# Splitting the turns of chunks 2 and 3 in a fused attention and expert kernel, with the copies of turned blocks put first on ACT

## Chip, cores and metric

The kernel runs on one core of one Trainium2 chip. The metric is the device time of one execution in microseconds (us), as the median of several runs. Engines are named as in the profile: PE (matrix engine; PEld is its weight load), DVE, ACT, POOL, and SP, which issues the transfers.

## What is computed

Block-causal attention for 8 batches of 8 heads with 576 positions and 64 columns per head, in fp32, and behind it an expert layer on the 4608 x 512 result with a hidden width of 2048:

```python
scores = np.where(mask, scale * np.matmul(q, k.transpose(0, 1, 3, 2)), -1000000000.0)   # 64x64 blocks
attn = np.exp(scores - np.max(scores, axis=-1, keepdims=True))
attn = attn / (np.sum(attn, axis=-1, keepdims=True) + 1e-09)
x = np.matmul(attn, v)          # then (4608, 512)
h = x @ w_in
g = h * (1.0 / (1.0 + np.exp(-1.702 * h)))
out = (g @ w_out).astype(np.float32)
```

## The kernel before

**Attention.** Two heads make a pair, and 32 pairs are worked off one after the other. A turn n (counted from 0, as in the code) does the scores of pair n and the end of pair n-1. The rows of a pair are cut into five chunks: chunk 0 has 64 rows and 64 columns, chunks 1 to 4 have 128 rows and 192, 320, 448 and 576 columns. `score` (L305) multiplies on PE into PSUM banks. `weigh` (L340) takes the row maximum on DVE (L351), which also moves the scores out of the bank, and the exponential on ACT (L358). `normalise` (L364) forms the reciprocal of the sums on DVE (L368, L371) and scales on POOL (L376).

**Turning.** The weights of attention must be transposed before they meet the values in `av` (L429). For pairs 0 to 7 PE transposes 128x128 blocks into a bank (`flip`, L401, through L102), and ACT copies them to `pw` (L411 for whole blocks, L424 for the 64-column ends). From pair 8 on DVE transposes (L385, L390) and transfers move the blocks. `flip` of chunks 2 and 3 is the step B, of chunk 4 the step C, of chunks 0 and 1 the step a.

**Banks.** All these products use PSUM banks in rotation (`bank`, L89). In turns 4 to 8, once the experts have begun, there are three, w0 to w2. A new writer waits until the reader of the bank's last contents is done: the maximum for scores, the copy for turned blocks. B takes four banks in a row: one for chunk 2, two for chunk 3, one for the ends.

**Experts.** 12 tiles of 384 tokens, and 16 hidden chunks of 128 in each. A chunk is 12 matmuls into the one bank of `hp` (four triples: w_in high, w_in low, and w_in high with the low part of x), the gate (ACT L562, DVE L563, ACT L571, POOL L82), and 9 matmuls of the chunk before into `acc`. The first tile lies between the steps of turns 4 to 8, and PE works in the order in which the program was written.

**Weights.** The two expert weights arrive as 64-bit words and are converted to a high and a low part in 32 pieces, in turns up to 8. Each piece goes ACT L219 into a bank, DVE L223, L229 and L234, ACT L243 (high part), POOL L82 (low part, `wil` or `wol`); the next piece begins after L243. Hidden chunks 12 to 15 need pieces 24 to 27 of w_in, one for each of the four triples.

**Order.** The slots of a turn are written out in strings (L26 to L33): `START` for turn 4, `ORDER[1]` for turns 5 to 7, `HANDOVER` for turn 8. Between the slots `advance` puts as much expert work as a quota by position asks for. On DVE, ACT and POOL a scheduler orders by priority; within `tc.high_priority(offset=300)` work goes ahead, before the change only for the gate and the split of x.

Of the kernel before, what the change touches and what calls it, by code (L numbers as in the profile page):

```python
# [24 lines left out]

ORDER = (  # L26
# [3 lines left out]
)  # L30

START = "1+0 - B 2/3 L C - V - 4 - a - - -"
HANDOVER = "B C - 3+0/2+1 - - V - - - 4 - - L - -"  # L33


WEIGHTS_BY = ((0, 0), (8, 13), (14.5, 32))
# [4 lines left out]
def attention_moe_kernel(  # L41
# [9 lines left out]
    nc = tc.nc  # L51
    B, H, S, D = q.shape
# [11 lines left out]
    HP = H // 2  # L64
# [9 lines left out]
    def early(n):  # L74

        return n < 2 * HP

    def phase(n):
        return 0 if n < HP else 1 if n < 2 * HP else 2
# [9 lines left out]
    def bank():  # L89
        tags = ["w0", "w1", "w2"]  # L90
        if not turns["experts"]:
            tags += ["acc0", "acc1", "acc2", "h"]
        elif turns["n"] > 2 * HP:
            tags.append("w3")
        turns["bank"] += 1
        return ps.tile([P, 512], F32, tag=tags[turns["bank"] % len(tags)], name="bank")
# [4 lines left out]
    def tr(**kw):  # L101
        return tc.keep_in_program_order(nc.tensor.transpose(**kw))  # L102
# [62 lines left out]
    def width(i):  # L165
        return BLK * (2 * i + 1)
# [46 lines left out]
    bits, whole = {}, {}  # L213
# [54 lines left out]
    def load(n):  # L268

        if n in (1, 3):  # L270
            raw[n] = room("xh", [P, 2, S // 32, 32], F32, "raw")
        else:
            raw[n] = d2.tile([P, 2, S // 32, 32], F32, tag="raw", name="raw", bufs=1)
        for x, src in enumerate((q, k)):
            queue = nc.scalar if n < 2 and x else nc.sync
            for hd, b, h in heads(n):
                for c in range(0, D, 32):
                    r = hd * D + c
                    queue.dma_start(
                        out=raw[n][r : r + 32, x],  # L280
                        in_=src[b, h][:, c : c + 32].rearrange("(c p) d -> p c d", p=32),
                    )
# [9 lines left out]
    def prep(n):  # L292

        tag = "e0" if early(n) and n % 2 else "qk"
        qk[n] = d2.tile([P, 2, S], F32, tag=tag, name="qk", bufs=1)
        for x in range(2):
            nc.vector.transpose(out=qk[n][:, x], in_=raw[n][:, x].rearrange("p c d -> p (c d)"))  # L297
        raw.pop(n)
        m = follower(n)
        if m is not None:  # L300
            load(m)
# [3 lines left out]
    def score(n, banks):  # L305

        if n not in stats:
            mx = d2.tile([P, NCH + 1, 2], F32, tag="mx", name="mx")
            sm = d2.tile([P, NCH, 2], F32, tag="sm", name="sm")
            stats[n] = (mx, sm)  # L310
        todo = []
        for chunks in banks:

            part = []
            for lo, hi in ((0, 512),) if width(chunks[0]) <= 512 else ((0, 256), (256, S)):
                ss = [bank() for _ in range(2)]
                c = 0
                for i in chunks:
                    a, z = qrange(i)
                    w = min(hi, width(i)) - lo  # L320
                    for hd in range(2):
                        r = slice(hd * D, hd * D + D)

                        mm(
                            out=ss[hd][:, c : c + w], lhsT=qk[n][r, 0, a : a + P],
                            rhs=qk[n][r, 1, lo : lo + w], start=True, stop=True,
                        )
                        part.append((i, hd, lo, lo + w, ss[hd][0 : z - a, c : c + w]))
                    c += w
            todo.append(sorted(part, key=lambda x: (chunks[::-1].index(x[0]), x[2])))  # L330
        for chunks, part in zip(banks, todo):
            e = {}
            for i, hd, lo, hi, s in part:
                e[i] = weigh(n, i, hd, lo, hi, s, e.get(i))
            for i in chunks[::-1]:
                normalise(n, i, e[i])
                if not early(n):
                    turn(n, i, e[i])
# [59 lines left out]
                        out=pw[kb * 32 : kb * 32 + 32, qb, 0:ns], in_=tw[qb * 32 : qb * 32 + 32, kb, 0:ns]  # L398
                    )

    def flip(n, chunks):  # L401

        for i in chunks:
            todo = [(j, hd) for j in range(i) for hd in range(2)]
            for x in range(0, len(todo), 4):
                part = todo[x : x + 4]
                bk = bank()
                for y, (j, hd) in enumerate(part):
                    tr(out=bk[:, y * P : (y + 1) * P], in_=es[i][:, hd, j * P : (j + 1) * P], identity=ident)
                s0 = SLOT[i] + part[0][0]  # L410
                nc.scalar.copy(  # L411
                    out=pw[:, :, s0 : s0 + len(part) // 2].rearrange("p b s h c -> p (s h) b c"),
                    in_=bk[:, 0 : len(part) * P].rearrange("p (x b c) -> p x b c", b=4, c=32),
                )

        bk = bank()
        todo = [(i, hd) for i in chunks for hd in range(2)]
        for y, (i, hd) in enumerate(todo):
            tr(out=bk[0:BLK, y * P : (y + 1) * P], in_=es[i][:, hd, i * P : width(i)], identity=ident)
        src = bk[0:BLK, 0 : len(todo) * P].rearrange("p (x b c) -> p x b c", b=4, c=32)  # L420
        for part in ([0], [1]) if 0 in chunks else (chunks,):
            i, x, a = part[0], 2 * chunks.index(part[0]), 2 if part[0] else 0
            s0 = 9 + max(i, 1)
            nc.scalar.copy(  # L424
                out=pw[0:BLK, a : a + 2, s0 : s0 + len(part)].rearrange("p b s h c -> p (s h) b c"),
                in_=src[:, x : x + 2 * len(part), a : a + 2],
            )

    def av(n):  # L429

        b, h = divmod(n, HP)
        before_av(n)
        o, o0 = bank(), bank()

        todo = []
        for i in range(1, NCH):
            c = (i - 1) * P
            todo += [(o, c, P, j, pw[:, :, SLOT[i] + j]) for j in range(i)]
            todo.append((o, c + BLK, BLK, i, pw[:, 2:4, 9 + i]))
        last = len(todo) - 1  # L440
        todo.append((o0, 0, BLK, 0, pw[:, 0:2, 10]))

        for x, (bk, c, nn, j, w) in enumerate(todo):
            for hd in range(2):
                mm(
                    out=bk[hd * D : hd * D + D, c : c + nn].rearrange("d (a c) -> d a c", c=32),
                    lhsT=values(n)[:, hd, j], rhs=w[:, :, hd], start=x in (0, last + 1), stop=x >= last,
                )
        c0 = (b % 2) * S
        nc.scalar.copy(out=xr[:, h, c0 : c0 + BLK], in_=o0[:, 0:BLK])  # L450
        nc.scalar.copy(out=xr[:, h, c0 + BLK : c0 + S], in_=o)
        m = follower(n)
        if m is not None:
            load_v(m)

    def follower(n):

        m = {0: 2, 1: 3, 2: 4, 3: None}.get(n, n + 1)
        return None if m is None or m >= NPAIR else m

    def order(n):
        return {HP: START, 2 * HP: HANDOVER}.get(n, ORDER[phase(n)]).split()

    def step(n):

        turns["n"] = n
        now = n < NPAIR

        def item(x):
            if x == "V":  # L470
                return (lambda: av(n - 1)) if n else None
            if x == "L":
                return (lambda: prep(n + 1)) if n + 1 < NPAIR else None
            if x in ("a", "B", "C"):
                m, chunks = {"a": (n, [0, 1]), "B": (n - 1, [2, 3]), "C": (n - 1, [4])}[x]
                return (lambda: flip(m, chunks)) if m >= 0 else None
            return (lambda: score(n, [[int(z) for z in y.split("+")] for y in x.split("/")])) if now and x != "-" else None

        return [item(x) for x in order(n)]
# [26 lines left out]
    def chunk_time(tt):  # L506
        return 4 * unit1(tt) + tt // P * 650
# [72 lines left out]
    ends = np.cumsum([0.0] + [NFC * chunk_time(tt) for _, tt in TILES])  # L580
# [84 lines left out]
```

## Time and profile before

| | us |
|---|---|
| median of 3 runs | 1122.48 (1120.67 to 1125.02) |
| profiled execution | 1120.49 |
| its span, first to last instruction | 1118.6 |
| PE busy | 1076.4 |
| DVE, ACT, POOL busy | 583.0, 498.6, 406.7 |

A busy share is an average over stages with different limits. A stretch of the span is read by its own row, and the idle time in front of an instruction, with what ended it, says who was late there. The granted clock is that of PE; 1.00 is 2.4 GHz and 0.50 is 1.2 GHz.

### The profile page before, as it was taken

How to read it: one execution, taken by the hardware profiler on the slowest of the kernel's cores; microseconds unless marked ns; L12 is line 12 of the kernel's file. 1: busy time of each engine (PE TensorE's matmuls, PEld its weight loads, DVE VectorE, ACT ScalarE, POOL GpSimd, SP SyncE). 2: the span in 40 equal slices, each digit the busy share in tenths (PEclk: the TensorE clock that was granted, in tenths of full speed). 3: DMA queues.
4: the chain of work that ended last, by engine and by line, in shares of the span. 5: the costliest groups of instructions: out<-in, count | busy, mean ns of one | idle time of the engine just before them, and what ended most of it. 6: DMA issues, size and time to landing. Idle time of an engine off the chain costs nothing. (4 is left out here: it accounts for less than half of the span.)

```text
span 1118.6 us, 19977 instructions
## 1 busy us (share of the span) xinstructions
PE 1076.4 (96%) x6960; PEld 908.7 (81%) x6960; DVE 583.0 (52%) x1856; ACT 498.6 (45%) x1321; POOL 406.7 (36%) x509
## 2 busy tenths in 40 slices
PE   5969998999999999999999999999999999999998
PEld 3757776788888888888888888888888888899997
DVE  6776885545545555654555655645545654211210
ACT  5866776434534433534443543444434444322322
POOL 4665664333333332333333333333333233122222
PEclk9979999999999999999999999999999999999999
DMA  8734532332444432343443333344342332200000
GB/s 171 205 89 153 150 73 62 84 79 57 105 86 86 103 80 64 64 98 78 98 101 74 75 93 65 70 108 85 81 107 63 71 85 58 54 29 1 29 1 29
DMA packets 219365, 91.25 MB, mean 82 GB/s; under 512 B 197760, under 2 KB 197760, under 8 KB 219264
## 3 DMA queue, kind: packets, MB, share of 16 engines
q1 hardware_dynamic: 214528, 89.38, 34.0%
q10 hardware_dynamic: 4736, 0.59, 0.3%
q8 instruction: 55, 0.90, 0.3%
q14 instruction: 46, 0.38, 0.1%
HBM read 45.09 MB, written 9.44 MB: 49 GB/s over the span
## 5 line engine op out<-in xcount | busy, mean ns | idle before, releaser
L82 POOL TENSOR_TENSOR gl<-g,gh 128x384 fp32r<-128x384 f32 x192 | 194.7, 1014 | 551.5 <-ACT gh L571 449.1
L99 PE MATMUL hp<-xh,wih 128*128 128x384 f32 x768 | 264.7, 345 | 7.9 <-DVE g L563 6.9
L563 DVE SCALAR_TENSOR_TENSOR g<-g,hp 128x384 f32<-128x384 f32 x192 | 105.9, 552 | 319.1 <-ACT g L562 317.8
L99 PE MATMUL hp<-xh,wil 128*128 128x384 f32 x768 | 258.4, 336 | 0.1
L562 ACT ACTIVATE g<-hp 128x384 f32<-128x384 f32 x192 | 94.1, 490 | 359.8 <-PE hp L99 354.8
L99 PE MATMUL hp<-xl,wih 128*128 128x384 f32 x768 | 253.9, 338 | 0.4 <-DVE xl L82 0.4
L99 PE MATMUL acc<-woh,gh 128*128 128x512 f32 x576 | 233.9, 406 | 0.0
L99 PE MATMUL acc<-wol,gh 128*128 128x512 f32 x576 | 226.9, 394 | 0.0
L99 PEld LDWEIGHTS hp<-xh,wih 128*128 128x128 f32 x768 | 144.2, 188 | 34.1 <-DVE g L563 23.1
L99 PE MATMUL acc<-woh,gl 128*128 128x512 f32 x576 | 167.9, 393 | 0.3 <-POOL gl L82 0.3
L571 ACT CAST gh<-g 128x384 fp32r<-128x384 f32 x192 | 98.4, 513 | 156.5 <-DVE g L563 156.4
L99 PEld LDWEIGHTS hp<-xh,wil 128*128 128x128 f32 x768 | 144.3, 188 | 6.5 <-POOL wil L82 0.7
L358 ACT ACTIVATE e<-e,mx 64x64 f32<-64x64 f32 (+4 forms) x240 | 132.3, 552 | 37.6 <-DVE mx L351 37.6
L376 POOL TENSOR_TENSOR e<-e,sm 64x64 f32<-64x64 f32 (+1 forms) x192 | 113.6, 612 | 95.0 <-DVE sm L371 46.5
L99 PEld LDWEIGHTS hp<-xl,wih 128*128 128x128 f32 x768 | 143.6, 188 | 1.3 <-DVE xl L82 1.3
L99 PE MATMUL bank<-qk 64*128 64x320 f32 (+4 forms) x768 | 122.5, 428 | 14.5 <-DVE qk L297 11.1
L99 PEld LDWEIGHTS acc<-woh,gh 128*128 128x128 f32 x576 | 107.9, 187 | 34.2 <-issue 10.5
L99 PEld LDWEIGHTS acc<-woh,gl 128*128 128x128 f32 x576 | 107.8, 188 | 25.9 <-POOL gl L82 1.2
L99 PEld LDWEIGHTS acc<-wol,gh 128*128 128x128 f32 x576 | 108.3, 188 | 16.7 <-POOL wol L82 0.3
L351 DVE CUSTOM_DVE_ANT_0 e<-bank,mask 64x64 f32<-64x64 f32 (+4 forms) x240 | 89.7, 417 | 56.9 <-PE bank L99 52.8
L385 DVE STREAM_TRANSPOSE turned<-e 128x384 f32<-128x384 f32 (+1 forms) x192 | 92.3, 499 | 48.8 <-POOL e L376 48.3
L99 PEld LDWEIGHTS bank<-qk 64*128 64x128 f32 x768 | 69.6, 193 | 54.2 <-issue 25.4
(50 smaller groups left out, 956.0 us busy)
## 6 DMA issues: line engine op xcount, KB each, us to landing
turned<-turned SPq DMA_DIRECT2D x192, 80.0 KB, 2.1
turned<-turned SPq DMA_DIRECT2D x96, 112.0 KB, 2.2
raw<-in_q_dram SPq DMA_DIRECT2D x128, 72.0 KB, 2.4
out_dram<-osb SPq DMA_DIRECT2D x36, 256.0 KB, 2.2
raw<-in_k_dram SPq DMA_DIRECT2D x120, 72.0 KB, 2.6
turned<-turned SPq DMA_DIRECT2D x96, 88.0 KB, 2.1
words<-in_moe_w_in_dram SPq DMA_DIRECT2D x16, 512.0 KB, 6.3
vp<-in_v_dram SPq DMA_DIRECT2D x60, 128.0 KB, 2.4
```

The costliest lines, as they stand in the source:

```text
L82: eng.tensor_tensor(out=out, in0=in0, in1=in1, op=ALU.subtract)
L99: return tc.keep_in_program_order(nc.tensor.matmul(**kw))
L351: nc.vector.tensor_tensor_reduce(out=e[0:m, hd, lo:hi], in0=s, in1=mk, op0=ALU.add, op1=ALU.min, scale=-0.125, scalar=3e38 if lo == 0 else ...
L358: nc.scalar.activation(out=e[0:m, hd], in_=e[0:m, hd], func=AF.Exp, scale=-1.0, bias=mx[0:m, i, hd : hd + 1], accum_out=sm[0:m, i, hd : hd ...
L376: nc.gpsimd.tensor_tensor(out=x, in0=x, in1=sc.to_broadcast([m, width(i)]), op=ALU.mult)
L385: nc.vector.transpose(out=tw[:, :, SLOT[i] : SLOT[i] + i, hd].rearrange("p b j c -> p j b c"), in_=e[:, hd, 0 : i * P],)
L562: nc.scalar.activation(out=g, in_=hp[:, 0:tt], func=AF.Tanh, scale=1.702)
L563: nc.vector.scalar_tensor_tensor(out=g, in0=g, scalar=1.0, in1=hp[:, 0:tt], op0=ALU.add, op1=ALU.mult)
L571: nc.scalar.copy(out=gh, in_=g)
```

## The change

Turns 5 to 8, the sixth to the ninth, get other steps. B is cut in two: b turns the whole blocks of chunk 2 and the ends of chunks 2 and 3 (two banks), c the whole blocks of chunk 3 (two banks), with experts in the slots between. In turn 8 C stands two slots behind c. The strings get longer, from 16 to 17 and from 16 to 19 slots, so the quota places expert work by finer steps. The copies of `flip` are issued at high priority for pairs from 4 on; that holds for a, b, c and C.

```diff
-    "1+0 - B - 2 - C - 3 L V - a - 4 -",
+    "1+0 - b - c 2 - C - 3 L V - a - 4 -",
-HANDOVER = "B C - 3+0/2+1 - - V - - - 4 - - L - -"
+HANDOVER = "b - c - C - 3+0/2+1 - - V - - - 4 - - L - -"
...
-    def flip(n, chunks):
+    def flip(n, chunks, whole=None, ends=True):
+        def move(**kw):
+            with tc.high_priority(offset=300 if n >= HP else 0):
+                nc.scalar.copy(**kw)
-        for i in chunks:
+        for i in chunks if whole is None else whole:
...
-                nc.scalar.copy(
+                move(
...
+        if not ends:
+            return
...
+            if x in ("b", "c"):
+                return lambda: flip(n - 1, [2, 3], [2] if x == "b" else [3], x == "b")
```

Lines behind the new code move: a copy at L411 or L424 becomes L407, the gate's L563 becomes L573.

**Turn 5, step B on PE** (the pieces of turns 6 and 7 look alike; `bank<-ident,turned` is a transpose, `hp` and `acc` are experts):

```order
 L99 MATMUL acc_988<-woh,gl 128x512
 L99 MATMUL acc_989<-woh,gl 128x512
-L102 MATMUL bank<-ident,turned 128x128 x10
+L102 MATMUL bank<-ident,turned 128x128 x4
 L102 MATMUL bank<-ident,turned 64x128 x4
 L99 MATMUL hp<-xh,wih 128x384
```

Six of the ten whole blocks leave this place; they come back three triples later.

**Turn 7, hidden chunk 12 on PE, before and after** (`hp_1925` and `hp_1913` are its bank, `wil` the low part of w_in; the transposes are C):

```order
L102 MATMUL bank_1940<-ident_64,turned_75 128x128 x4
L102 MATMUL bank_1946<-ident_64,turned_75 128x128 x4
L102 MATMUL bank_1952<-ident_64,turned_75 64x128 x2
L99 MATMUL hp_1925<-xh_977,wih_1571 128x384
L99 MATMUL hp_1925<-xh_977,wil_1572 128x384
L99 MATMUL hp_1925<-xl_978,wih_1571 128x384
```

```order
L99 MATMUL hp_1913<-xh_977,wih_1574 128x384
L99 MATMUL hp_1913<-xh_977,wil_1575 128x384
L99 MATMUL hp_1913<-xl_978,wih_1574 128x384
L102 MATMUL bank_1943<-ident_64,turned_75 128x128 x4
L102 MATMUL bank_1949<-ident_64,turned_75 128x128 x4
L102 MATMUL bank_1955<-ident_64,turned_75 64x128 x2
```

The chunk's last triple stood behind C and stands ahead of it now.

**The same place on POOL, before and after** (`wil` of pieces 25 to 27; `turned<-turned,sm` scales a chunk, 64x64 chunk 0, 128x192 chunk 1, 128x320 chunk 2):

```order
L82 TENSOR_TENSOR gl<-g,gh 128x384
L376 TENSOR_TENSOR turned<-turned,sm 64x64
L376 TENSOR_TENSOR turned<-turned,sm 128x192 x2
L82 TENSOR_TENSOR wil<-wm,wih 128x512 x2
L376 TENSOR_TENSOR turned<-turned,sm 128x320 x2
L82 TENSOR_TENSOR gl<-g,gh 128x384
```

```order
L82 TENSOR_TENSOR wil<-wm,wih 128x512
L376 TENSOR_TENSOR turned<-turned,sm 128x192 x2
L82 TENSOR_TENSOR gl<-g,gh 128x384
L82 TENSOR_TENSOR wil<-wm,wih 128x512
L376 TENSOR_TENSOR turned<-turned,sm 128x320 x2
L82 TENSOR_TENSOR wil<-wm,wih 128x512
L82 TENSOR_TENSOR gl<-g,gh 128x384
```

The low parts of pieces 26 and 27 stood in a row ahead of chunk 2's scaling; now piece 27's stands behind it.

**And on DVE** (`wm_1727` is what L234 makes of piece 27; L351 are the maxima of chunk 2):

```order
L223 TENSOR_SCALAR wm_1721<-wm_1721 128x512
L229 SCALAR_TENSOR_TENSOR wm_1721<-words_1575,wm_1721 128x512
L351 ISA turned_75,mx_1817<-bank_1913,mask_69 128x320
L351 ISA mx_1817 128x1
L234 SCALAR_TENSOR_TENSOR wm_1727<-words_1575,wm_1721 128x512
L351 ISA turned_75,mx_1817<-bank_1914,mask_69 128x320
L351 ISA mx_1817 128x1
L297 STREAM_TRANSPOSE qk_1999<-raw_1655 128x576
```

```order
L234 SCALAR_TENSOR_TENSOR wm_1646<-words_1578,wm_1624 128x512
L351 ISA turned_75,mx_1817<-bank_1917,mask_69 128x320
L351 ISA mx_1817 128x1
L351 ISA turned_75,mx_1817<-bank_1918,mask_69 128x320
L351 ISA mx_1817 128x1
L223 TENSOR_SCALAR wm_1673<-wm_1673 128x512
L297 STREAM_TRANSPOSE qk_1999<-raw_1658 128x576
L229 SCALAR_TENSOR_TENSOR wm_1673<-words_1578,wm_1673 128x512
L368 TENSOR_SCALAR sm_1818<-sm_1818 128x2
L234 SCALAR_TENSOR_TENSOR wm_1727<-words_1578,wm_1673 128x512
L371 RECIPROCAL sm_1818<-sm_1818 128x2
```

Piece 27's three steps were woven into the maxima, and now stand behind both, with L297 and L368 between.

**Turn 8, the handover, on PE**:

```order
 L99 MATMUL acc_988<-woh,gl 128x512
 L99 MATMUL acc_989<-woh,gl 128x512
+L99 MATMUL hp<-xh,wih 128x384
+L99 MATMUL hp<-xh,wil 128x384
+L99 MATMUL hp<-xl,wih 128x384
+L102 MATMUL bank<-ident,turned 128x128 x6
+L99 MATMUL hp<-xh,wih 128x384
+L99 MATMUL hp<-xh,wil 128x384
+L99 MATMUL hp<-xl,wih 128x384
```

One triple, chunk 3's blocks and three more triples, of which the first is shown, now stand between b and C.

## Rows read from the trace of the kernel before

**Rows 1.** Page, part 1: busy us, share of the span, instructions.

```profile
PE 1076.4 (96%) x6960; PEld 908.7 (81%) x6960; DVE 583.0 (52%) x1856; ACT 498.6 (45%) x1321; POOL 406.7 (36%) x509
```

**Rows 2.** Stretches: us, PE busy (instructions), granted clock, DMA share, GB/s.

```profile
84.00:112.00 28.00, 26.58 (x146) 1.00 0.49 153
112.00:140.00 28.00, 26.23 (x189) 1.00 0.58 151
140.00:168.00 28.00, 27.38 (x192) 1.00 0.31 72
168.00:196.00 28.00, 24.08 (x192) 1.00 0.25 62
```

**Rows 3.** PE in time, step B, turns 5 to 7: start, us, instruction [idle].

```profile
100.58 0.63 PE L102 MATMUL bank<-ident,turned 128*64 128x128 f32 x4 [1.42 <-ACT turned L411]
...
129.40 0.63 PE L102 MATMUL bank<-ident,turned 128*64 128x128 f32 x4 [1.60 <-ACT turned L411]
...
157.62 0.63 PE L102 MATMUL bank<-ident,turned 128*64 128x128 f32 x4 [0.46 <-ACT turned L411]
```

**Rows 4.** PE in time, turn 8.

```profile
181.60 1.90 PE L102 MATMUL bank<-ident,turned 128*128 128x128 f32 x14
...
185.97 0.33 PE L102 MATMUL bank<-ident,turned 128*128 128x128 f32 x1 [1.07 <-POOL turned L376]
188.30 1.20 PE L102 MATMUL bank<-ident,turned 128*128 128x128 f32 x9 [2.00 <-POOL turned L376]
...
199.44 0.34 PE L99 MATMUL bank<-turned,vp 128*64 128x64 f32 x4 [1.52 <-DVE mx L351]
```

**Rows 5.** PE's weight loads in time, hidden chunk 12 in turn 7.

```profile
162.62 0.19 PEld L99 LDWEIGHTS hp<-xh,wil 128*128 128x128 f32 x1 [0.47 <-POOL wil L82]
...
164.44 0.19 PEld L99 LDWEIGHTS hp<-xh,wil 128*128 128x128 f32 x1 [0.18 <-POOL wil L82]
```

**Rows 6.** DVE's instructions in time, chunk 2 and one piece in turn 6.

```profile
133.23 0.49 DVE L351 CUSTOM_DVE_ANT_0 turned<-bank,mask 128x320 f32<-128x320 f32 x1 [0.30 <-PE bank L99]
...
135.96 0.70 DVE L223 TENSOR_SCALAR wm<-wm 128x512 uint32<-128x512 uint32 x1
...
138.19 0.69 DVE L234 SCALAR_TENSOR_TENSOR wm<-words,wm 128x512 uint32<-128x512 uint32 x1
```

**Rows 7.** DVE's instructions in time, the gate in turn 6.

```profile
126.70 0.56 DVE L563 SCALAR_TENSOR_TENSOR g<-g,hp 128x384 f32<-128x384 f32 x1 [0.32 <-ACT g L562]
```

**Rows 8.** POOL's instructions in time, turn 6, up to piece 19.

```profile
125.84 2.25 POOL L376 TENSOR_TENSOR turned<-turned,sm 128x576 f32<-128x576 f32 x2 [1.96 <-DVE mx L351]
...
131.69 1.27 POOL L82 TENSOR_TENSOR wil<-wm,wih 128x512 fp32r<-128x512 f32 x1
```

**Rows 9.** PE in time, turn 6: scores of chunk 2, piece 19's triple.

```profile
132.39 0.81 PE L99 MATMUL bank<-qk 64*128 64x320 f32 x4
...
133.77 0.34 PE L99 MATMUL hp<-xh,wih 128*128 128x384 f32 x1
```

**Rows 10.** POOL's instructions in time, piece 27 and chunk 2 in turn 7.

```profile
163.11 1.28 POOL L82 TENSOR_TENSOR wil<-wm,wih 128x512 fp32r<-128x512 f32 x1 [0.54 <-ACT wih L243]
165.05 1.40 POOL L376 TENSOR_TENSOR turned<-turned,sm 128x320 f32<-128x320 f32 x2 [0.66 <-PE hp L99]
```

**Rows 11.** Short stretches, columns as in rows 2.

```profile
16.00:20.00 4.00, 4.00 (x24) 0.57 0.70 134
...
60.00:62.00 2.00, 0.04 (x1) 0.60 0.79 127
...
66.00:70.00 4.00, 3.67 (x8) 0.50 0.89 286
...
72.00:74.00 2.00, 2.00 (x19) 0.50 0.00 0
...
186.00:188.00 2.00, 0.30 (x1) 1.00 0.00 0
```

More of the change, by code (lines that the diff above doesn't have):

```diff
@@ L423, in flip @@
             s0 = 9 + max(i, 1)
-            nc.scalar.copy(
+            move(
                 out=pw[0:BLK, a : a + 2, s0 : s0 + len(part)].rearrange("p b s h c -> p (s h) b c"),
```

## The prediction, made before the change ran

> **What bounds the kernel now.** I began with the busy times: PE is busy for 1076.4 of 1118.6 us [rows 1], so a shorter run needs PE to idle less. Then I looked for the stretch in which the edited steps run, turns 5 to 8, from about 84 to 205 us. The stretch table shows the idle time that can be won: 28.00 less PE's busy time is 1.42, 1.77, 0.62 and 3.92 us, together 7.7 us from 84 to 196 [rows 2]. Outside that stretch the order on PE does not change, up to a place or two in turn 9. So the change moves a few us at most, and each wait in the stretch has to be followed on its own. The reader is to see four kinds.
>
> The first is a bank. B's ends wait 1.42, 1.60 and 0.46 us for a copy on ACT in turns 5, 6 and 7 [rows 3]: they need a fourth bank, and three rotate. The second is the handover: C waits 1.07 and 2.00 us for POOL to scale chunk 4, and the last four matmuls of `av` wait 1.52 us for a row maximum on DVE [rows 4]. The third is small and easily overlooked: in turn 7 the weight loads of hidden chunk 12 wait 0.47 and 0.18 us for the low part of w_in on POOL [rows 5]. Weights reach PE there just in time, so whatever makes PE earlier in turns 5 to 7, or the weights later, is paid at that place. The fourth is the clock, below.
>
> **The change part by part.** The sum is made against the profiled execution of 1120.49 us, of which 1.89 us lie outside the span; the median is 1.99 us above it. I carry the difference over to the median.
>
> The fourth bank. With b and c apart, the ends are the second bank that b takes, and c's banks are asked for three triples later, after b's first copy, which now goes first on ACT. The three waits go: -1.42 - 1.60 - 0.46 = -3.48 us. I see nothing that would keep them.
>
> What is late next there. The ends now use the bank of the first head's scores of chunks 0 and 1, so they wait for chunk 1's maximum on DVE. In the built order of turn 5 the last weight step, 0.69 us long [rows 6], stands ahead of that maximum, and the piece starts later, because its first ACT step moved behind the gate: 0.65 us. In turn 6 the gate itself stands ahead of it; it ended at 127.26 [rows 7]. The ends came up at 129.40 - 1.60 = 127.80 [rows 3], and six blocks of 1.90 / 14 = 0.14 us [rows 4] no longer precede them, so they come up at 127.0 and find the maximum, a third of a us behind the gate, at 127.6: 0.55 us. Together +1.2 us, between 0 and 2.1 (PE comes later, or nothing on DVE moves forward with it). The split itself costs nothing that I can see: 14 transposes take 1.90 us and 9 take 1.20 [rows 4], which leaves no fixed part.
>
> Piece 19 in turn 6. POOL worked without a break from 125.84 to 132.96 on two scalings of chunk 4, a low part, a gate, four small scalings and piece 19's low part [rows 8]. The same work still stands in front of it, with the low part first. PE's triple with piece 19 began at 133.77 [rows 9]. By the terms so far PE would come there 1.42 - 0.65 + 1.60 - 0.55 = 1.8 us earlier, at 131.9. POOL has the piece at 132.96 if nothing changes, which makes a wait of 1.1 us; with copies and exponentials now ahead of the ACT step that releases the low part before it, I take POOL 0.9 us later: +2.0 us, between 1.1 and 2.6.
>
> Piece 27 in turn 7, the largest term. Copies that go first on ACT push the weights' casts back, and the built order shows it: piece 27's DVE steps stand behind both maxima of chunk 2, and on POOL its low part stands behind chunk 2's scaling. On PE, the triple that needs it has moved ahead of C. So the time from the start of chunk 2's scores to that low part can be added up. From the scores' start to the first maximum: 133.23 - 132.39 = 0.84 us [rows 6, 9]. Two maxima of 0.49 us, less overlap: 0.9. The six DVE instructions L223, L368, L297, L229, L371 and L234 took 138.88 - 135.96 = 2.92 us in turn 6 [rows 6]; here they are the same ones in another order. About 0.3 us to POOL. Scaling 1.40 and the low part 1.28 us [rows 10]. That is 7.6 us. PE needs 133.77 - 132.39 = 1.38 us for the scores and one triple [rows 9]; here two triples and one matmul stand before the load, some 2.1 us. PE waits 7.6 - 2.1 = 5.5 us, of which 0.65 is paid already [rows 5]: +4.9 us. Without the scaling in front it would be 3.5; with piece 26's low part, 1.28 us as well, late on top, 6.2.
>
> The handover. In the built order four triples stand between b's experts and C that were not there. At about 0.55 us each they cover 2.2 of the 3.07 us [rows 4]. POOL also has no low part between the two scalings of chunk 4 any more; I leave 0.7 us of the wait. The triple between the scores and `av` is among those four, so the wait of 1.52 us, which hangs on the scores' start, grows by 0.55. Sum -3.07 + 0.7 + 0.55 = -1.8 us, between -2.5 and -0.5.
>
> The waits alone: -3.48 + 1.2 + 2.0 + 4.9 - 1.8 = +2.8 us.
>
> The clock. The granted clock is 1.00 in all of the stretch [rows 2], but ahead of it, after long waits, it fell: 0.60 from 60 to 62 us with PE busy for 0.04 us, and still 0.50 from 66 to 70 and from 72 to 74 with PE busy nearly throughout; another time it was 0.57 from 16 to 20 [rows 11]. At 0.50 PE is at 1.2 GHz. In the handover PE was busy for only 0.30 of 2 us and kept 1.00 [rows 11]. The wait in chunk 12 is 5.5 us or more with a few matmuls in it, more like the first case than the last. The price: 0.43 x 4.00 = 1.7 us by the row from 16 to 20, and half of 3.67 + 2.00 + 2.00, 3.8 us, by those up to 74 (70 to 72 was as full). Dense expert work follows here, as from 16 to 20; I take +2.2 us. The Trainium skill (TensorE: Matmul & The Clock Gate, What's actually happening) says of the gate that "the default state is throttled, and activity releases the throttle", and that it follows how busy PE has been recently. By that rule this change pays for its stall twice, and the sum is +5.0 us; without it +2.8. The trace agrees with a fall behind a long wait, and shows in the handover that not every wait brings one.
>
> Together +2.8 + 2.2 = +5.0 us: 1122.48 + 5.0 = **1127.5 us** (1125.5 for an execution like the profiled one).
>
> **The rivals.** First, the weights keep pace, and only the waits named by the edit change: -3.48 + 1.2 - 1.8 = -4.1 us, 1118.4 us. For it: PE is the bound nearly everywhere, and the weights' steps are short beside its work. Against it: the order on POOL and DVE above, and that the weights are just in time already [rows 5]. It decides from the point where piece 27's low part is done within 2.1 us of the scores' start.
>
> Second, the change does not do what it says, because the weights set PE's time in chunk 12 in both versions. Everything won in turns 5 to 7 is then waited off there and nothing is added; the handover's -1.8 stays: 1120.7 us. For it: its two waits there [rows 5]. Against it: the chain gets longer in the built order, not only visible.
>
> Third, the stall as above, but the clock stays at 2.4 GHz: +2.8 us, 1125.3 us. For it: 186 to 188 us [rows 11]; against it: 60 to 62 [rows 11].
>
> Fourth, all at the upper ends, with pieces 28 to 31 dragging on into the handover: -3.48 + 2.1 + 2.6 + 6.2 - 0.5 + 3.8 = +10.7 us, 1133.2 us.
>
> **How the numbers follow.** My forecast 0.40, clock stays 0.25, nothing but the handover 0.15, weights keep pace 0.13, upper ends 0.07. A measurement of this kernel can tell about 0.5%, 5.6 us, from no change, so the bounds are 1116.9 and 1128.1 us. Faster: a part of the case that the weights keep pace, with more won at the handover, 0.07. Slower: somewhat under half of the forecast's 0.40 (0.17), a little of the case with the clock high (0.04) and the upper ends (0.07), 0.28. The same: 0.65. The range of 8 in 10 leaves out the upper ends beyond 1131.5 and the better half of the case that the weights keep pace, below 1118. The forecast's own range, from the bounds of its terms, is 1124 to 1132 us.
>
> **What would show it.** No idle time before b, c or the ends that a copy on ACT ended: the first term is right. Half a us before the ends that a maximum on DVE ended, in turns 5 and 6: the second. Weight loads of `hp` with `wil` that wait about 2 us for POOL in turn 6 and about 5 us in turn 7: the third and fourth; if they wait under 1 us in turn 7, the forecast is wrong and the first rival is right. A granted clock near 0.50 behind that wait: the clock term. C's wait for POOL under 1 us and the tail of `av` near 2 us: the handover. Idle time in the turns behind turn 9 that was not there before would be something that I have not seen.

## The result and the profile after

The changed kernel took 1127.36 us (median of 10 runs, 1126.32 to 1131.24), the kernel before 1123.38 us in as many runs beside it (1120.67 to 1125.16). The ratio is 1.0039, interval 1.0025 to 1.0052: 4.0 to 4.4 us more. The profiled execution took 1129.88 us, its span 1127.9. PE was busy for 7 us longer, 1083.4 against 1076.4 us [rows 1], with as many instructions: some ran at a lower clock, as shown below. Part 1 of the page after:

```profile
PE 1083.4 (96%) x6960; PEld 916.0 (81%) x6960; DVE 584.3 (52%) x1856; ACT 499.7 (44%) x1321; POOL 406.7 (36%) x509
```

The same four stretches as [rows 2] (us, PE busy, instructions, granted clock, DMA share, GB/s):

```profile
84.00:112.00 28.00, 27.67 (x150) 0.99 0.49 153
112.00:140.00 28.00, 25.43 (x177) 0.94 0.57 147
140.00:168.00 28.00, 25.41 (x178) 1.00 0.28 62
168.00:196.00 28.00, 25.63 (x166) 0.88 0.33 76
```

The first stretch gained busy time, the next two lost it, and the clock is no longer 1.00 throughout. PE in time, every wait from 97 to 212 us of over 0.15 us (start, length, instruction, and in brackets the idle time ahead of it with what ended it):

```profile
100.04 0.60 PE L102 MATMUL bank<-ident,turned 128*64 128x128 f32 x4 [0.33 <-DVE mx L351]
121.56 0.80 PE L99 MATMUL bank<-qk 64*128 64x320 f32 x2 [0.35 <-DVE mx L351]
127.90 0.60 PE L102 MATMUL bank<-ident,turned 128*64 128x128 f32 x4 [0.53 <-DVE sm L371]
134.91 0.44 PE L99 MATMUL hp<-xh,wil 128*128 128x384 f32 x1 [1.69 <-POOL wil L82]
164.53 0.44 PE L99 MATMUL hp<-xh,wih 128*128 128x384 f32 x1 [0.19 <-ACT wih L243]
165.88 0.45 PE L99 MATMUL hp<-xh,wil 128*128 128x384 f32 x1 [0.91 <-POOL wil L82]
168.50 0.45 PE L99 MATMUL hp<-xh,wih 128*128 128x384 f32 x1 [2.00 <-ACT wih L243]
170.71 0.69 PE L99 MATMUL hp<-xh,wil 128*128 128x384 f32 x1 [1.76 <-POOL wil L82]
197.27 1.21 PE L102 MATMUL bank<-ident,turned 128*128 128x128 f32 x9 [0.61 <-POOL turned L376]
201.12 1.10 PE L99 MATMUL bank<-qk 64*128 64x320 f32 x6 [0.85 <-DVE mx L351]
207.20 0.34 PE L99 MATMUL bank<-turned,vp 128*64 128x64 f32 x4 [2.19 <-DVE mx L351]
```

No idle time ends at a copy on ACT any more, so the three waits of [rows 3] are gone. Their place is taken by matmuls of `hp` that wait for weights: 1.69 us in turn 6, and 0.19 + 0.91 + 2.00 + 1.76 = 4.86 us in hidden chunk 12 in turn 7. In the handover the two waits of [rows 4] for POOL have become one of 0.61 us, and the tail of `av` waits for 2.19 us instead of 1.52. The eleven rows sum to 11.41 us; the kernel before had ten such waits, 9.46 us.

Behind three of these waits the clock fell. Short stretches, columns as above:

```profile
134.00:136.00 2.00, 1.09 (x5) 0.97 0.88 307
136.00:138.00 2.00, 2.00 (x7) 0.50 0.25 102
138.00:140.00 2.00, 2.00 (x12) 0.68 0.23 37
...
170.00:172.00 2.00, 1.29 (x5) 0.50 0.12 8
172.00:174.00 2.00, 2.00 (x10) 0.50 0.60 160
174.00:176.00 2.00, 2.00 (x6) 0.50 0.34 93
176.00:178.00 2.00, 2.00 (x8) 0.79 0.96 242
...
208.00:210.00 2.00, 2.00 (x6) 0.50 0.56 128
210.00:212.00 2.00, 2.00 (x9) 0.76 0.01 3
```

Busy time times one less the clock is an estimate of the time lost: 0.03 + 1.00 + 0.64 = 1.7 us behind piece 19, 0.65 + 1.00 + 1.00 + 0.42 = 3.1 us behind chunk 12, and 1.00 + 0.48 = 1.5 us behind the tail of `av`. POOL in turn 7, where the long wait is made:

```profile
161.11 1.29 POOL L82 TENSOR_TENSOR wil<-wm,wih 128x512 fp32r<-128x512 f32 x1
...
164.55 1.27 POOL L82 TENSOR_TENSOR wil<-wm,wih 128x512 fp32r<-128x512 f32 x1 [0.26 <-ACT wih L243]
168.04 1.39 POOL L376 TENSOR_TENSOR turned<-turned,sm 128x320 f32<-128x320 f32 x2 [2.22 <-DVE sm L371]
169.40 1.26 POOL L82 TENSOR_TENSOR wil<-wm,wih 128x512 fp32r<-128x512 f32 x1
```

The last row is piece 27. It stands behind chunk 2's scaling, and the scaling waits 2.22 us for a reciprocal on DVE (L371 at 167.72 us) that came behind the last of the piece's three steps there (L234 at 167.11 us).

### The profile page after: what moved, and what is told of

It is laid out like the page before. It is cut to its first block, busy times and chain, and to the rows that moved or that the text cites. A ratio compares the mean times of both kernels' runs of the same rounds, so it can differ in the third digit from the quotient of the medians.

```text
span 1127.9 us, 19971 instructions
## 1 busy us (share of the span) xinstructions
PE 1083.4 (96%) x6960; PEld 916.0 (81%) x6960; DVE 584.3 (52%) x1856; ACT 499.7 (44%) x1321; POOL 406.7 (36%) x509
## 4 chain that ended last, share of the span: by engine, by line
PE 58%; DVE 1%; SPq 1%; issue 1%; ACT 0%; DMA 0%; POOLq 0%; POOL 0%; DVEq 0%; ACTq 0%
PE hp L99 24%; PE acc L99 24%; PE bank L99 9%; SPq L397 1%; ACT e L358 0%; DMA turned<-turned 0%; DVE turned L385 0%; DVE e L378 0%; DVE e L351 0%; DVE g L573 0%; POOLq L670 0%; DVE turned L390 0%; ACT osb L538 0%; ACT gh L581 0%; ACT g L572 0%
## 5 line engine op out<-in xcount | busy, mean ns | idle before, releaser
L573 DVE SCALAR_TENSOR_TENSOR g<-g,hp 128x384 f32<-128x384 f32 x192 | 106.1, 552 | 332.2 <-ACT g L572 330.8
L351 DVE CUSTOM_DVE_ANT_0 e<-bank,mask 64x64 f32<-64x64 f32 (+4 forms) x240 | 89.8, 417 | 55.5 <-PE bank L99 51.4
```

The costliest lines, as they stand in the source:

```text
L351: nc.vector.tensor_tensor_reduce(out=e[0:m, hd, lo:hi], in0=s, in1=mk, op0=ALU.add, op1=ALU.min, scale=-0.125, scalar=3e38 if lo == 0 else ...
L573: nc.vector.scalar_tensor_tensor(out=g, in0=g, scalar=1.0, in1=hp[:, 0:tt], op0=ALU.add, op1=ALU.mult)
```

## The experiments

The change has three parts: copies that go first on ACT, B cut in two in turns 5 to 7, and the longer handover. Medians in us; each ratio is against runs of the kernel before on the same chip. The first four, the next four and the last four kernels ran on one chip each.

| kernel | copies first | B cut | handover | median | ratio, interval |
|---|---|---|---|---|---|
| after_again | yes | yes | new | 1127.20 | 1.0047 (1.0034 to 1.0060) |
| prio_only | yes | no | old | 1129.67 | 1.0068 (1.0056 to 1.0080) |
| split_only | no | yes | new | 1118.73 | 0.9968 (0.9956 to 0.9980) |
| turns_only | yes | yes | old | 1129.35 | 1.0066 (1.0051 to 1.0082) |
| prio_early | turns 5, 6 | yes | new | 1125.90 | 1.0026 (1.0015 to 1.0037) |
| prio_late | from turn 7 | yes | new | 1121.22 | 0.9987 (0.9978 to 0.9996) |
| keep_busy | yes | yes | new | 1128.10 | 1.0043 (1.0027 to 1.0058) |
| split_weights_ahead | no | yes | new | 1122.18 | 0.9996 (0.9986 to 1.0007) |
| keep_busy_half | yes | yes | new | 1126.31 | 1.0024 (1.0012 to 1.0035) |
| after_third | yes | yes | new | 1126.98 | 1.0038 (1.0023 to 1.0053) |
| split_turns_only | no | yes | old | 1123.21 | 0.9995 (0.9985 to 1.0006) |
| split_again | no | yes | new | 1119.93 | 0.9962 (0.9949 to 0.9975) |

### The changed kernel twice more

Expected of after_again: 

> The changed kernel once more, for a second profile. In the first one PE waited 1.69 us for piece 19 and 0.19 + 0.91 + 2.00 + 1.76 = 4.86 us for pieces 26 and 27, and the granted clock fell to 0.50 behind both. Theory (the waits come from the order of the program, and the clock falls behind them): the same waits within 0.3 us each, the clock at or near 0.50 behind chunk 12's again, 1126 to 1128 us. Rival (the first profile was one of several courses that the same order can take): waits that differ by more than 1 us, or a clock that stays at 1.00 behind them.

Expected of after_third: 

> The changed kernel, to stand beside the run with 21 unread matmuls: 1126.5 to 1128 us, with the clock at 0.50 behind chunk 12.

Each wait came back within 0.3 us: 1.66 us for piece 19 in both, together 4.44 and 4.76 us in chunk 12. The clock behind chunk 12 fell both times, at a loss of 2.0 and 2.5 us. Behind piece 19 it fell in the second profile (1.7 us lost) and not in the third, behind the tail of `av` in neither. So the theory held for the waits, and its rival in part for the clock. One more thing shows when profiles are laid side by side. The last scores ahead of turn 5 began at 85.97 us in the profile of the kernel before, at 87.18, 87.39 and 87.33 in the three of the changed kernel, and at 86.09 to 89.30 in the ten other kernels below. PE's order up to that place is the same in all of them, so the executions differ there by more than the edits explain, and the profiled one of before is the earliest: 1.2 to 1.4 us of the difference were made ahead of the edit.

### Which part costs: copies first, or the split

```diff
-    "1+0 - b - c 2 - C - 3 L V - a - 4 -",
+    "1+0 - B - 2 - C - 3 L V - a - 4 -",
-HANDOVER = "b - c - C - 3+0/2+1 - - V - - - 4 - - L - -"
+HANDOVER = "B C - 3+0/2+1 - - V - - - 4 - - L - -"
```

Expected of prio_only: 

> The old turns (B in one piece, the old handover); only the copies of pairs 4 and later go first on ACT. Theory (the copies' place on ACT pushes the weights back): piece 27's low part again stands behind chunk 2's scaling in POOL's order, PE waits 2 to 5 us in chunk 12, and the ends still need a fourth bank, but wait less for it: 1123 to 1126 us. Rival (the split, which brings PE earlier, makes the wait): under 1 us of wait in chunk 12, 1121 to 1122.5 us.

```diff
-            with tc.high_priority(offset=300 if n >= HP else 0):
+            with tc.high_priority(offset=0):
```

Expected of split_only: 

> The split turns and the new handover, with the copies at their old place in the order. Theory (the copies' place on ACT): piece 27's low part stands ahead of chunk 2's scaling in POOL's order, so PE waits 1 to 3 us in chunk 12, and 1121 to 1124 us. Rival (the split): chunk 12 waits 4 to 5 us as with both, 1126 to 1128 us.

The two answers are far apart: with the copies first alone the kernel is slower by 0.7%, with the split alone faster by 0.3%. PE's waits in turn 5 and in chunk 12 with the copies first alone:

```profile
100.62 1.28 PE L102 MATMUL bank<-ident,turned 128*128 128x128 f32 x10 [0.32 <-DVE mx L351]
...
165.94 0.44 PE L99 MATMUL hp<-xh,wih 128*128 128x384 f32 x1 [2.05 <-ACT wih L243]
168.87 0.69 PE L99 MATMUL hp<-xh,wil 128*128 128x384 f32 x1 [2.48 <-POOL wil L82]
172.93 0.69 PE L99 MATMUL hp<-xh,wih 128*128 128x384 f32 x1 [0.92 <-ACT wih L243]
174.27 0.69 PE L99 MATMUL hp<-xh,wil 128*128 128x384 f32 x1 [0.66 <-POOL wil L82]
```

Two things are read here. The B steps of turns 5 to 7 wait for no copy, although B is whole and its ends need a fourth bank: copies that go first free the banks in time. So either part removes the waits of [rows 3], and together they do it twice. And chunk 12 waits 2.05 + 2.48 + 0.92 + 0.66 = 6.1 us for weights, more than with the split. I had expected 2 to 5 us and 1123 to 1126 us; it was worse than that. With the split alone no wait over 0.15 us stands ahead of b or the ends in turn 5, and chunk 12 shows:

```profile
164.55 0.45 PE L99 MATMUL hp<-xh,wil 128*128 128x384 f32 x1 [0.67 <-POOL wil L82]
```

Chunk 12 waits 0.67 us, below the 1 to 3 us that I expected, and the time is below the 1121 to 1124 us. The difference between 0.67 and 4.86 us is the copies' place on ACT.

### Which copies

```diff
-            with tc.high_priority(offset=300 if n >= HP else 0):
+            with tc.high_priority(offset=300 if HP < turns["n"] <= 6 else 0):
```

Expected of prio_early: 

> The split as in the changed kernel; the copies go first on ACT in turns 5 and 6 only, and stand at their old place from turn 7 on. In the built order POOL has piece 27's low part behind chunk 2's scaling in turn 7, as with all copies first. Theory (the copies of turns 5 and 6 set the weights back by a piece, and PE pays in turn 7): 4 to 5 us of waits in chunk 12 with the clock at 0.50 behind them, 1126 to 1128 us. Rival (the copies of turn 7 itself hold piece 27 up): under 2 us of waits in chunk 12, 1119 to 1121 us.

The mirror has `turns["n"] >= 7` as its condition.

Expected of prio_late: 

> The mirror of the one before: the copies go first on ACT from turn 7 on only. Piece 27's low part stands ahead of chunk 2's scaling on POOL. Theory (turns 5 and 6): as with the split alone, at most 1 us of waits in chunk 12, 1118 to 1120 us. Rival (turn 7): 4 to 5 us there, 1126 to 1128 us.

With the copies of turns 5 and 6 first, PE waits in turn 7 as in the changed kernel, and the clock falls behind it as there; the time, 1125.90 us, is just below the 1126 to 1128 us expected:

```profile
163.67 0.44 PE L99 MATMUL hp<-xh,wil 128*128 128x384 f32 x1 [0.91 <-POOL wil L82]
166.29 0.45 PE L99 MATMUL hp<-xh,wih 128*128 128x384 f32 x1 [2.00 <-ACT wih L243]
168.49 0.69 PE L99 MATMUL hp<-xh,wil 128*128 128x384 f32 x1 [1.75 <-POOL wil L82]
```

With those from turn 7 on first, chunk 12 waits 0.54 + 0.91 = 1.45 us, somewhat above the 1 us of the theory, and the time is 2.5 us above split_only's median, 0.2% by the ratios; the 1118 to 1120 us of the theory were missed by that. Where all of these 2.5 us come from isn't shown; in this profile the clock fell behind the tail of `av` (1.7 us lost), in split_only's it didn't. The larger part of the cost is made in turns 5 and 6. There piece 20's low part falls behind chunk 2's scaling on POOL; the changed kernel in turn 6:

```profile
138.29 1.40 POOL L376 TENSOR_TENSOR turned<-turned,sm 128x320 f32<-128x320 f32 x2
140.78 1.28 POOL L82 TENSOR_TENSOR wol<-wm,woh 128x512 fp32r<-128x512 f32 x1 [1.09 <-ACT woh L243]
```

With the split alone it stands ahead of that scaling, which begins at 139.73 us:

```profile
136.04 1.27 POOL L82 TENSOR_TENSOR wol<-wm,woh 128x512 fp32r<-128x512 f32 x1 [1.85 <-ACT woh L243]
```

The stream of weights never makes the place good and enters turn 7 a piece late. POOL in turn 7 with the split alone, to be laid beside the changed kernel's rows in the section on the result:

```profile
157.06 1.29 POOL L82 TENSOR_TENSOR wil<-wm,wih 128x512 fp32r<-128x512 f32 x1
...
159.91 1.29 POOL L82 TENSOR_TENSOR wil<-wm,wih 128x512 fp32r<-128x512 f32 x1
...
163.22 1.28 POOL L82 TENSOR_TENSOR wil<-wm,wih 128x512 fp32r<-128x512 f32 x1
```

These are the low parts of pieces 25, 26 and 27, done at 164.50. In the changed kernel the rows at 161.11, 164.55 and 169.40 are the same pieces, and 27 is done at 170.66.

### What the handover is worth

```diff
-HANDOVER = "b - c - C - 3+0/2+1 - - V - - - 4 - - L - -"
+HANDOVER = "B C - 3+0/2+1 - - V - - - 4 - - L - -"
```

Expected of turns_only (copies first): 

> Everything as in the changed kernel, but with the old handover (B, then C right behind it). It prices the handover: C waits 2 to 3 us again for the scaling of chunk 4, and the last matmuls of av wait 0.5 us less. Theory (the handover gives 1 to 2 us back): 1128 to 1130 us. Rival (what the handover wins is lost to the clock or to a later wait): the same as the changed kernel within 0.5 us.

Expected of split_turns_only (the same edit, copies at their old place): 

> The split of turns 5 to 7 with the copies at their old place, and the old handover. It prices the handover without the stalls ahead of it. Theory (the handover gives 1.5 to 2.2 us by itself): C waits 2.5 to 3.1 us for the scaling of chunk 4, the last matmuls of av 1.5 us, and the time is 1.5 to 2.2 us above the split with the new handover, 1120 to 1121 us. Rival (most of the gain lies in the handover, not in the turns): 1122 to 1123 us, no better than the kernel before.

Expected of split_again: 

> The split with the new handover, copies at their old place, once more beside the others: 1118 to 1120 us, 3 to 4.5 us below the kernel before.

With the copies first the new handover is worth 2.15 us (1129.35 to 1127.20), a little above the 1 to 2 us expected. Without them it is worth 3.3 us (1123.21 to 1119.93; 0.33% by the ratios), and the split of turns 5 to 7 by itself is worth nothing: 0.9995 of the kernel before. There my theory failed and the rival was right. PE with the split turns and the old handover:

```profile
127.73 0.60 PE L102 MATMUL bank<-ident,turned 128*64 128x128 f32 x4 [0.53 <-DVE sm L371]
134.74 0.45 PE L99 MATMUL hp<-xh,wil 128*128 128x384 f32 x1 [1.22 <-POOL wil L82]
151.96 0.80 PE L99 MATMUL bank<-qk 64*128 64x320 f32 x2 [1.03 <-DVE mx L351]
165.02 0.45 PE L99 MATMUL hp<-xh,wil 128*128 128x384 f32 x1 [0.68 <-POOL wil L82]
...
187.27 0.33 PE L102 MATMUL bank<-ident,turned 128*128 128x128 f32 x1 [1.09 <-POOL turned L376]
189.60 2.18 PE L102 MATMUL bank<-ident,turned 128*128 128x128 f32 x9 [1.99 <-POOL turned L376]
```

The 3.48 us of [rows 3] are gone, and 0.53 + 1.22 + 1.03 + 0.68 = 3.46 us have come in their place. PE that is earlier meets a normalisation, two pieces of weights and a maximum that are no earlier. With the new handover C waits 0.29 us instead of 3.08. The profile with the old handover also shows the clock at 0.50 from 190 to 194 us, behind these two waits:

```profile
190.00:192.00 2.00, 2.00 (x11) 0.50 0.00 0
192.00:194.00 2.00, 2.00 (x8) 0.50 0.00 0
```

The kernel before kept 1.00 behind the same waits in its profile [rows 11]. With the copies first and the old handover (turns_only) C waits 1.81 + 0.78 us, and there the clock fell as well, to 0.57 and 0.58 from 196 to 200 us. How often it does, profiles of single executions don't tell.

### Whether the clock falls for want of work

```diff
                 for cnt, (wa, xb, dc) in enumerate(terms):
+                    [mm(out=hp[:, TT:512], lhsT=ident, rhs=ident, start=False, stop=False)
+                     for _ in range({(12, "wil", 2, False): 8, (12, "wih", 3, False): 18, (12, "wil", 3, False): 16}
+                                    .get((fc, wa, dc, xb is xl), 0) if t == 0 else 0)]
```

Expected of keep_busy: 

> The changed kernel with 42 matmuls added that nobody reads, in hidden chunk 12 of the first tile: 8 ahead of the matmul that waits for piece 26's low part, 18 and 16 ahead of those that wait for piece 27's high and low part. The weights come no earlier. Theory (the clock falls because PE stands idle in those waits): the added matmuls fill 2 to 4.5 of the 4.5 to 4.9 us, the granted clock stays at 1.00 behind them instead of 0.50 for 6 us, and the time is 2 to 3 us below the changed kernel, 1124 to 1125.5 us. Rival (the clock falls there whatever PE does): still 0.50 behind chunk 12, 1127 us or, if the added matmuls take longer than the waits, more.

Expected of keep_busy_half (4, 9 and 8): 

> The changed kernel with 21 unread matmuls in hidden chunk 12 in place of 42: 4, 9 and 8 ahead of the three that wait. In the run with 42 each took 0.21 us (two of 0.107), together 9 us against 4.4 us of waits, so PE came 3.9 us later to the last of the three, though the clock stayed at 1.00. With 21 they take 0.86, 1.93 and 1.72 us against waits of 0.91, 2.00 and 1.52 to 1.76. Theory (the clock costs what the stretch table shows): PE is later by at most 0.3 us, the clock stays at 1.00 behind chunk 12, and the time is 1 to 3 us below that of the changed kernel on the same chip. Rival (the clock is no PE time, since the weights bound that stretch anyway): the same as the changed kernel within 0.5 us.

With 42 added matmuls the clock stayed at 1.00 behind chunk 12, but they took 1.95 + 4.18 + 3.73 = 9.9 us, twice the waits that they filled, and the time didn't fall: 1.0043 of the kernel before, against 1.0038 to 1.0047 without filler. The expectation of the time was wrong because I hadn't sized the filler. With 21 the fit is close. PE in chunk 12 (each added matmul counts as two), and the stretches behind it:

```profile
163.80 1.05 PE L99 MATMUL hp<-ident 128*128 128x128 f32 x8
...
165.32 2.17 PE L99 MATMUL hp<-ident 128*128 128x128 f32 x18
...
167.78 1.95 PE L99 MATMUL hp<-ident 128*128 128x128 f32 x16
```

```profile
168.00:170.00 2.00, 2.00 (x17) 1.00 0.00 0
170.00:172.00 2.00, 2.00 (x16) 1.00 0.52 158
```

From the first matmul of `av` in turn 6 to that in turn 7 this kernel took 32.97 us, after_third 35.22 in the same stretch. That is 2.25 us, close to the 2.5 us that the stretch table shows as lost there; after and after_again took 35.81 and 34.35 us, with 3.1 and 2.0 us lost. After_third had no fall behind piece 19 inside it, while this profile had one just ahead of it. Of the whole time little of that is left: 0.7 us by the medians, 1.6 us by the ratios, whose intervals overlap. Of the six profiles in which 4.4 to 6.1 us of waits stand unfilled in chunk 12 (the three of the changed kernel, prio_only, turns_only and prio_early) the clock fell behind them in all. So it is shown that the clock falls behind these waits because PE has nothing to do, and that the stretch pays for it; what a median gets back by filling them isn't settled. The Trainium skill (TensorE: Matmul & The Clock Gate, What's actually happening) has activity release the throttle, and the two kernels with filler agree: 1.00 where the same waits unfilled gave 0.50 in each of the three profiles.

### Weights ahead of everything

In the split without copies first, the weights' steps of pieces 16 to 27 were put 50 places forward:

```diff
-            if odd:
-                split_weights(j)
...
+            with tc.high_priority(offset=50 if 16 <= j <= 27 else 0):
+                if odd:
+                    split_weights(j)
...
```

Expected of split_weights_ahead: 

> The split and the new handover with the copies at their old place, and the steps of pieces 16 to 27 of the weights moved forward by 50 places in the order's priorities. In the built order pieces 25 to 27 come 1 to 3 places earlier on POOL, piece 19 stays. Theory (what is left of the waits for weights, 0.67 us in chunk 12 with the split alone, is PE time): 0.5 to 0.7 us below the split alone, 1118 us. Rival (something else is late next, a maximum on DVE behind the weights' steps): 1118.7 to 1121 us.

The rival was right in kind, though 1122.18 us lies above its range, too. Chunk 12's wait fell to 0.15 us, but the steps that gave way are now late:

```profile
150.98 0.63 PE L102 MATMUL bank<-ident,turned 128*64 128x128 f32 x4 [1.57 <-ACT xr L459]
155.93 1.43 PE L99 MATMUL bank<-qk 64*128 64x320 f32 x2 [1.57 <-DVE mx L351]
```

Behind the second wait the clock was 0.50 from 156 to 162 us, at a loss of 3.4 us. How much of this is in the median isn't known: the profiled execution took 1126.15 us and is the slowest of twelve. It is the same lesson as that of the copies with the parts changed over: on ACT and DVE each step put first pushes another one back that PE waits for. split_only is the fastest kernel here, 0.32% and 0.38% below the kernel before on two chips.

## Why the prediction was right, and where it was not

1127.5 us was forecast and 1127.36 measured. That the two agree so closely is luck: the change was forecast as +5.0 us and measured as +4.0 to +4.4, and the median of the kernel before was 1123.38 us beside the changed kernel, 0.9 above the one that the sum was carried to. The terms were nearer than I had a right to expect all the same. Point by point:

- **The fourth bank, -3.48 us:** right, no wait for a copy is left. The step that the prediction didn't have is that either part of the change suffices for it, and that the gain of the split is paid back in the same turns even when the weights aren't pushed back at all (split_turns_only: 3.46 us for 3.48). This is the mechanism of the second rival, that the weights set PE's time; with the maxima it holds in all of turns 5 to 7, not in chunk 12 alone.
- **The ends, +1.2 us:** 0.33 + 0.53 = 0.86 us. In turn 6 the reciprocal of the sums on DVE (L371) ended the wait, not a maximum.
- **Piece 19, +2.0 us:** 1.66 to 1.69 us.
- **Piece 27, +4.9 us:** the chain from the start of chunk 2's scores (162.81) to the matmul with the low part (170.71) took 7.9 us, where I had added up 7.6. It came as three waits and a bit: piece 26's low part was late, too, and piece 27's high part was waited for by itself, 2.00 us, which I hadn't listed. Together 4.44 to 4.86 us, less the 0.65 that were counted as paid before: +3.8 to +4.2 us, inside the bounds of 3.5 to 6.2. That 0.65 was too much to take off: it is idle time of the weight loads, and on PE itself neither wait of before reaches 0.15 us.
- **Why piece 27 is late:** I named the copies that go first on ACT, and that is shown. Where they do it I had too narrow: I read the order of turn 7, and the piece is mostly lost in turns 5 and 6 (prio_early, prio_late).
- **The handover, -1.8 us:** C's wait went from 3.07 to 0.61 us (0.7 was forecast), the tail grew by 0.67 (0.55); the scores ahead of `av` wait 0.35 us longer, which I hadn't seen. That makes -1.4 us in the trace; the kernels gave -2.15 with the copies first and -3.3 without, where the waits of each pair of profiles make -1.0 and -2.4. A term that fits what is left is the clock behind the old waits: I took its 1.00 from the one profile that I had, and it fell in turns_only (1.4 us lost) and split_turns_only (2.7). With one profile of each that isn't settled.
- **The clock, +2.2 us:** 3.1, 2.0 and 2.5 us behind chunk 12. I had no fall behind piece 19, which cost 1.7 us in two of three profiles, and none behind the tail of `av`, 1.5 us in one.
- **The sum:** the waits were +1.9 to +2.2 us instead of +2.8, and the clock +2.5 to +6.3 instead of +2.2. Against that, 1.2 to 1.4 us of the 1.99 by which the profiled execution was ahead of its median lay ahead of the edit, which speaks for carrying the difference over. From the scores at 86 to 87 us to the end of the span the three profiles are 8.1, 4.7 and 4.1 us longer than that of before; the first is the one with all three falls of the clock, 6.3 us.

Faster by over 0.5% or slower by over 0.5%: neither, as the largest chance had it. The rival with the weights keeping pace, 1118.4 us, did not happen, but the split gives nearly that time with the copies left at their place, 1118.73 and 1119.93 us. Its sum is met by luck there: the turns gave nothing in place of -2.3 us, and the handover -3.3 in place of -1.8.

## What to carry to other kernels

A step that is put first on an engine is paid for by the stream that stood there, and the bill comes where that stream was just in time: here a turn or two later and on another engine. When two edits remove the same wait, run them apart; here one was free and the other cost 7 to 9 us. And a wait that is removed in front of a chain of work that is just in time is only moved: add up what is late next until the idle time is found again or gone.

## What the runs showed of the hardware that I had not expected

The same wait doesn't always bring the clock down. The wait of 1.65 to 1.69 us for piece 19 stood in seven profiles; behind it the granted clock fell to 0.50 in four (after, after_again, turns_only, keep_busy_half) and stayed at 1.00 in three (after_third, prio_early, keep_busy). The 2.19 us ahead of the tail of `av` stood in ten profiles, all with the new handover; behind it the clock fell in three (after, prio_late, split_again). Behind the 3.1 us of the old handover it stayed in the profile of before and fell in that of split_turns_only. A time below half a per cent therefore has to be read from medians of several runs, and a single profile is good for the waits and not for the clock behind them.
